# Mirrored times made as pairs by three products instead of four, with the V pairs in six stages and the next batch's folds moved to other steps, in an FFT mixing and spatial gating kernel

## The chip, the cores and the metric

The kernel runs on one core of one Trainium2 chip. The metric is device time in microseconds (us) of one execution; less is better. TensorE is called PE below, its weight loads PEld, VectorE DVE, ScalarE ACT, GpSimd POOL and the queue that issues most loads SP. Times of kernels are medians of runs in the fast state: none is over 1.5% above the fastest of its kernel. The spans and traces come from one profiled run each.

## The reference, cut to what matters

```python
batch, seq, dim, d_ff = 8, 3072, 256, 1024
X = np.fft.fft(np.fft.fft(x, axis=1), axis=2).real        # x: (8, 3072, 256)
h = np.maximum(X @ w_in, 0.0)                             # (8, 3072, 1024)
u, v = h[..., :512], h[..., 512:]
v_n = (v - mean(v)) / sqrt(var(v) + 1e-6)                 # over the last axis
v_s = einsum('ts,bsd->btd', w_spatial, v_n) + b_spatial   # (3072 x 3072) over time
out = (u * v_s) @ w_out                                   # (8, 3072, 256)
```

The spatial product is by far the largest. The point of the change is a symmetry. The transform at time S-t differs from that at time t only in the sign of the part that is odd in the width direction. With E and O for the even and odd half (128 rows each) and W0, W1 for the matching halves of the transformed w_in, h(t) = E W0 + O W1 before the relu, and h(S-t) = E W0 - O W1. The kernel only ever makes E and O for half of the times.

## The kernel before

The parts that matter: V (the second half of h, normalised), U (the first half), the gate, and the place of the work for the next batch. A batch is 6 chunks of 512 times, each 4 tiles of W of 768 rows; each tile has 4 steps, one per 128 columns of V, so 96 steps of six 128x512 products. PSUM is the memory that PE's products land in, divided into banks. `psM` is a ring of four of its banks that all small products share; `psW` holds the four sums of a chunk.

```python
def v_tile(b, i, eo, v, pr):            # one of 24 tiles of 128 times
    pv = psM.tile([P, DH], FP32, name="pv", tag="psM")
    for kt in range(2):
        if i < 12:                      # a direct time
            l, w = eo[:, kt, 128 * i:128 * i + 128], weo[:, kt, DH:]
        else:                           # a mirrored time: odd weights negated (wom)
            s0 = 128 * (KT - 1 - i) + 1
            l = eo[:, kt, s0:s0 + 128]
            w = weo[:, 0, DH:] if kt == 0 else wom[:, DH:]
        nc.tensor.matmul(pv, lhsT=l, rhs=w, start=(kt == 0), stop=(kt == 1))
    nc.scalar.activation(out=r, in_=pv, func=AF.Relu)
    nc.vector.bn_stats(out=stt[:, jj, :], in_=r)
    nc.vector.bn_aggr(out=mv[:, jj, :], in_=stt[:, jj, :])
# ... root and norm once per two tiles ...

def u_tile(b, c, dt, eo):               # likewise two products for each of 24 tiles
    # ...
    nc.scalar.activation(out=ut, in_=pu, func=AF.Relu)

def gate(c, pw, ut):                    # in the fourth tile of every chunk, once per step
    nc.vector.tensor_tensor(out=tm, in0=pw, in1=bbc[:, TC * c:TC * c + TC], op=ALU.add)
    nc.vector.tensor_tensor(out=gt, in0=tm, in1=ut, op=ALU.mult)

# in prep(b): what batch b needs, laid into the tiles of batch b-1
f0, df = (3, 2) if b == 1 else (0, 3)
for a in range(NA):                     # three folds of x, each an even and an odd half
    steps[f0 + df * a][0].append(lambda a=a: s_even(a))    # tiles 0, 3, 6 (3, 5, 7 for b == 1)
    steps[f0 + df * a][2].append(lambda a=a: s_odd(a))
```

A fold adds and subtracts mirrored rows and columns of x, on DVE; the DCT then makes E and O from the folds by products with tables of sines. Four of the 3072 times are left out of the folds and come in as the specials' sums (spb). Batch 0 has a head of its own: the tables, the three folds, the specials' sums, the first W pieces (128 times by 768 columns of w_spatial; each cast to bf16, turned by PE, copied out of PSUM), the DCT, and the first V tiles ahead of the main loop.

## Time and profile before

| | before |
|---|---|
| time (median of the first three runs) | 1470.2 us |
| PE busy | 1372.1 us, 93% of the span |
| DVE, ACT, POOL busy | 740.0, 464.2, 133.7 us |
| PE's wait for the gate (tm) | 23.4 us in 8 waits |
| first spatial product | at 80.8 us |
| batch 0, from its first spatial product to batch 1's | 228.2 us |
| batches 1 to 6, each | 168.3 us on average |
| batch 7 | 144.5 us |

In the busy shares, read PE first: at 93% it is the bound, and the question is what it does and where it stops.

### The profile page before, as it was taken

The page shows a single profiled execution, that of the slowest core. Times are in us where ns is not written, and L with a number is a line of the kernel's source. Part 1 is how long each engine was busy: PE and PEld are TensorE (multiplying, and loading weights), DVE is VectorE, ACT ScalarE, POOL GpSimd, SP SyncE. Part 2 cuts the span into 40 slices and gives each one's busy share as a digit, 9 for nine tenths or more (in the row PEclk, how much of TensorE's full clock was granted, in tenths as well). Part 3 has the DMA queues.
Part 4 walks back from the last instruction along what each step waited for, and adds up shares of the span by engine and source line. Part 5 has one row for each costly group of instructions (what it writes and reads, how often), then busy time and mean ns, then how long its engine had stood idle before and what let it go on. Part 6 is the DMA issues. An engine that isn't in the chain of part 4 may idle for free.

```text
span 1471.1 us, 18005 instructions
## 1 busy us (share of the span) xinstructions
PE 1372.1 (93%) x7071; PEld 673.5 (46%) x7071; DVE 740.0 (50%) x1491; ACT 464.2 (32%) x779; POOL 133.7 (9%) x187
## 2 busy tenths in 40 slices
PE   0667999999999999999999999999999999999998
PEld 0333455544444444444444444444444444444444
DVE  6757745555355634655344733565345643561212
ACT  3554235521244123431244113431244212441111
POOL 7622434410000000000000000000000000000000
PEclk9878999999999999999999999999999999999999
DMA  7863999795333543346334463336344443434441
GB/s 258 282 223 125 329 337 297 259 330 180 129 129 126 196 163 124 122 141 224 122 129 133 151 203 129 129 122 228 130 138 141 151 159 122 144 127 157 143 158 50
DMA packets 100597, 255.28 MB, mean 174 GB/s; under 512 B 13568, under 2 KB 60192, under 8 KB 100384
## 3 DMA queue, kind: packets, MB, share of 16 engines
q1 hardware_dynamic: 61440, 196.66, 39.4%
q10 hardware_dynamic: 29568, 44.05, 8.2%
q0 software_dynamic: 9504, 13.42, 2.8%
q8 instruction: 55, 0.90, 0.2%
q14 instruction: 30, 0.25, 0.0%
HBM read 210.80 MB, written 56.62 MB: 182 GB/s over the span
## 4 chain that ended last, share of the span: by engine, by line
PE 84%; DVE 7%; ACT 1%; issue 1%; ACTq 0%; DVEq 0%
PE pw L496 63%; PE po L512 6%; PE pu L488 5%; PE pv L454 5%; DVE tm L501 2%; PE pt L151 1%; PE pe L408 1%; DVE gt L504 1%; DVE sm L308 1%; DVE xt L328 1%; DVE stt L458 1%; DVE of L330 0%; DVE ef L312 0%; ACT v_t L472 0%; ACT r L457 0%
## 5 line engine op out<-in xcount | busy, mean ns | idle before, releaser
L496 PE MATMUL pw<-wt,v_t 128*128 128x512 bf16 x4608 | 1084.5, 382 | 37.6 <-DVE tm L501 23.4
L496 PEld LDWEIGHTS <-v_t 128*128 128x128 bf16 x4608 | 451.6, 98 | 581.2 <-issue 41.3
L501 DVE TENSOR_TENSOR tm<-pw,bbc 128x512 f32<-128x512 f32 x192 | 131.0, 682 | 263.5 <-PE pw L496 263.5
L490 ACT ACTIVATE ut<-pu 128x512 bf16<-128x512 f32 x192 | 114.6, 597 | 318.0 <-PE pu L488 213.2
L458 DVE BATCH_NORM_STATS2 stt<-r 128x6 f32<-128x512 f32 x192 | 132.6, 690 | 162.0 <-ACT r L457 162.0
L516 ACT COPY ot<-po 128x512 f32<-128x512 f32 x96 | 56.3, 586 | 309.6 <-PE po L512 308.0
L504 DVE TENSOR_TENSOR gt<-tm,ut 128x512 bf16<-128x512 f32 x192 | 135.8, 707 | 13.8 <-DVE tm L501 0.5
L457 ACT ACTIVATE r<-pv 128x512 f32<-128x512 f32 x192 | 111.0, 587 | 100.5 <-PE pv L454 91.3
L472 ACT ACTIVATE v_t<-r,rs 128x512 bf16<-128x512 f32 x96 | 78.1, 813 | 105.1 <-DVE rs L470 104.4
L512 PE MATMUL po<-wob,gt 128*128 128x256 bf16 x768 | 103.6, 279 | 1.4 <-DVE gt L504 1.4
L488 PE MATMUL pu<-eo_t,weo 128*128 128x512 bf16 x288 | 95.1, 385 | 2.4 <-ACT r L457 2.4
L454 PE MATMUL pv<-weo,eo_t 128*128 128x512 bf16 x288 | 94.7, 385 | 0.8 <-DVE wt L154 0.3
L512 PEld LDWEIGHTS <-gt 128*128 128x128 bf16 x768 | 76.8, 101 | 32.4 <-issue 3.3
L156 ACT COPY wt<-pt 128x768 bf16<-128x768 bf16 x53 | 42.0, 800 | 61.4 <-PE pt L151 61.0
L469 DVE RECIPROCAL rs<-rs 128x2 f32<-128x2 f32 x96 | 15.5, 162 | 89.0 <-ACT rs L465 89.0
L151 PE MATMUL pt<-ident,wb 128*128 128x128 bf16 x576 | 50.6, 231 | 6.9 <-ACT r L457 2.8
L454 PEld LDWEIGHTS <-eo_t 128*128 128x128 bf16 x384 | 37.2, 100 | 41.8 <-issue 2.7
L151 PEld LDWEIGHTS <-wb 128*128 128x128 bf16 x576 | 42.4, 104 | 29.0 <-issue 7.0
L474 DVE TENSOR_SCALAR v_t<-r,mv,rs 128x512 bf16<-128x512 f32 x96 | 52.7, 549 | 0.0
L146 POOL CAST wb<-wr 128x768 bf16<-128x768 f32 x48 | 42.6, 895 | 78.4 <-PE pt L151 46.9
L143 POOL CAST wb<-wr 128x768 bf16<-128x768 f32 x48 | 42.1, 887 | 70.3 <-PE pt L151 40.2
L410 ACT ACTIVATE eo_t<-pe,spb 128x384 bf16<-128x384 f32 (+1 forms) x32 | 35.8, 1117 | 37.8 <-PE pe L408 37.8
(218 smaller groups left out, 664.2 us busy)
## 6 DMA issues: line engine op xcount, KB each, us to landing
wt<-wtd SPq DMA_DIRECT2D x168, 768.0 KB, 4.4
wr<-in_moe_w_spatial_dram SPq DMA_DIRECT2D x96, 384.0 KB, 5.2
out_dram<-ot ACTq DMA_DIRECT2D x96, 256.0 KB, 3.9
wtd<-wt ACTq DMA_DIRECT2D x24, 768.0 KB, 5.3
xr<-in_x_dram POOLq DMA_DIRECT2D x32, 384.0 KB, 11.7
xt<-in_x_dram SPq DMA_DIRECT2D x21, 512.0 KB, 4.0
xt<-xr SPq DMA_DIRECT2D x21, 512.0 KB, 5.0
x<-in_x_dram SPq DMA_DIRECT2D x1, 1536.0 KB, 6.6
```

Of the source, the lines that this page charges most:

```text
L151: nc.tensor.transpose(pt[:, kk, :], wb[:, 128 * kk:128 * kk + 128], ident)
L454: nc.tensor.matmul(pv, lhsT=l, rhs=w, start=(kt == 0), stop=(kt == 1))
L457: nc.scalar.activation(out=r, in_=pv, func=AF.Relu)
L458: nc.vector.bn_stats(out=stt[:, jj, :], in_=r)
L472: nc.scalar.activation(out=v[:, i - 1, :], in_=r2[0], func=AF.Identity, scale=rs[:, 0:1], bias=rs[:, 2:3])
L488: nc.tensor.matmul(pu, lhsT=w, rhs=r, start=(kt == 0), stop=(kt == 1))
L490: nc.scalar.activation(out=ut, in_=pu, func=AF.Relu)
L496: nc.tensor.matmul(pw, lhsT=v[:, k, 128 * dt:128 * dt + 128], rhs=wt[:, kk, :], start=(k == 0), stop=(k == KT - 1))
L501: nc.vector.tensor_tensor(out=tm, in0=pw, in1=bbc[:, TC * c:TC * c + TC], op=ALU.add)
L504: nc.vector.tensor_tensor(out=gt, in0=tm, in1=ut, op=ALU.mult)
L512: nc.tensor.matmul(po[:, i, :], lhsT=gts[dt][:, t0:t0 + 128], rhs=wob[:, dt, :], start=(dt == 0), stop=(dt == NDT - 1))
L516: nc.scalar.copy(out=ot, in_=po)
```

## The change

The change has two intents: to save products where PE is the bound, and to move the folds out of the steps in which the gates run. A mirrored pair is made together: pv = E W0 + O W1 as before, pd = O (2 W1) as a third product, and the mirror is pv - pd. So three products stand where four did. ACT copies pd to SBUF and DVE subtracts. In U the mirror's relu moves into the gate. A V pair is cut into six stages, one per step, so that ACT and DVE do not wait for each other inside a stage. Time S/2 has no mirror and gets small products of its own. W's columns and rows are reordered to fit. The folds of the next batch stand in new steps, none of them a gate's, and in the head the first nine W casts move from POOL to ACT.

```diff
-NWR = 6
+NWR = 5
+ORDER = [0, 3, 1, 4, 2, 5]
+FOLD = [(2, 4), (8, 16), (18, 20)]          # steps of the even and odd halves, of 96
+FOLD1 = [(16, 20), (22, 26), (32, 34)]      # the same for batch 1
+DCT = [36, 38, 40, 42]
+VAT = [44 + (17 * i) // 4 for i in range(NPAIR)]
 ...
+        src = wr if g % 2 == 0 else view(wr, HW - 1, [[-1, HW]])
+        if first:
+            nc.scalar.copy(out=wb, in_=src)
         else:
-            nc.gpsimd.tensor_copy(out=view(wb, 127, ...), in_=view(wr, 0, ...))
+            nc.gpsimd.tensor_copy(out=wb, in_=src)
 ...
+    def v_pair(i, eo, pr):
+        for kt in range(2):
+            nc.tensor.matmul(pv, lhsT=eo[:, kt, sl], rhs=weo[:, kt, DH:], ...)
+        nc.tensor.matmul(pd, lhsT=eo[:, 1, sl], rhs=wo2[:, DH:], start=True, stop=True)
+        nc.scalar.activation(out=r[0], in_=pv, func=AF.Relu)
+        nc.scalar.copy(out=m_, in_=pd)
+    def v_minus(i, eo, pr, pv, pd):
+        nc.vector.tensor_tensor(out=r[1], in0=pv, in1=pd, op=ALU.subtract)
+        nc.vector.bn_stats(out=stt[:, 0, :], in_=r[0])
+    # v_relu (ACT), v_stat (DVE), v_root (ACT), v_norm (both): one stage a step
 ...
+    def u_pair(c, dt, eo):       # the same three products; um = pu - m_, no relu
 ...
-        nc.vector.tensor_tensor(out=gt, in0=tm, in1=ut, op=ALU.mult)
+        nc.vector.scalar_tensor_tensor(out=gt, in0=ut, scalar=0.0, in1=tm, op0=ALU.max,
+                                       op1=ALU.mult)
 ...
+    sp_ = specials()             # its PE part and DVE copies now come after the folds
     for i in range(3):
         piece(True)
 ...
+    early = [[] for _ in range(3 * NPAIR + 6)]      # batch 0: two pairs interleaved
+    for i in range(NPAIR):
+        for n, f in enumerate(cur.v_steps(i)):
+            early[3 * i + n].append(f)
```

## The prediction

> **What bounds the kernel now.** I read the page's busy shares first, then its slices, the costliest groups, PE's own waits, and last the chain of waits over single stretches. The busy shares and slices of the kernel before:
>
> ```profile
> PE 1372.1 (93%) x7071; PEld 673.5 (46%) x7071; DVE 740.0 (50%) x1491; ACT 464.2 (32%) x779; POOL 133.7 (9%) x187
> ...
> PE   0667999999999999999999999999999999999998
> ...
> PEclk9878999999999999999999999999999999999999
> ```
>
> The first line gives each engine's busy time in a span of 1471.1 us; the other two give PE's busy tenths and its granted clock in 40 slices of 36.8 us. PE is full from the fifth slice on; DVE is half used and ACT a third. There are two regimes: a head of some 147 us in which PE starves, and a long PE-bound rest. The costliest group, and the groups that the change touches:
>
> ```profile
> L496 PE MATMUL pw<-wt,v_t 128*128 128x512 bf16 x4608 | 1084.5, 382 | 37.6 <-DVE tm L501 23.4
> ...
> L501 DVE TENSOR_TENSOR tm<-pw,bbc 128x512 f32<-128x512 f32 x192 | 131.0, 682 | 263.5 <-PE pw L496 263.5
> L490 ACT ACTIVATE ut<-pu 128x512 bf16<-128x512 f32 x192 | 114.6, 597 | 318.0 <-PE pu L488 213.2
> L458 DVE BATCH_NORM_STATS2 stt<-r 128x6 f32<-128x512 f32 x192 | 132.6, 690 | 162.0 <-ACT r L457 162.0
> ...
> L516 ACT COPY ot<-po 128x512 f32<-128x512 f32 x96 | 56.3, 586 | 309.6 <-PE po L512 308.0
> ```
>
> 382 ns is the time of one pipelined matmul, not its spacing. The spacing comes from the chain of waits over 320 to 345 us (start, length, what; a steady batch):
>
> ```profile
> 322.15 5.18 PE pw L496 x24
> 327.33 0.43 PE pu L488 x2
> ...
> 330.43 1.23 DVE sm L308
> ...
> 339.98 0.60 DVE tm L501
> 340.58 0.04 issue
> 340.62 2.72 PE pw L496 x6
> 343.33 1.14 PE po L512 x8
> 344.48 0.43 PE pu L488 x2
> 344.91 5.18 PE pw L496 x24
> ```
>
> 24 matmuls take 5.18 us, 0.216 us each: what one 128x512 product costs while PE is the bound. The DVE lines in the middle are the one recurring stall. The folds of x for the next batch (sm to ho, about 3.7 us for either half) stand in the step in which the first chunk's four gates run; the gates queue behind them, and a PSUM bank of the next chunk is not free. PE's own waits (waited for: us in total, times, longest):
>
> ```profile
> PE pw L496 <- DVE tm L501: 23.4, 8, 3.7
> PE pw L496 <- ACT v_t L472: 14.2, 7, 3.3
> ```
>
> The 8 DVE waits are 3.7 and 0.5 us in batch 0 and six of 3.2 us, one in each of batches 1 to 6. The ACT waits all lie between 83 and 133 us, in the head. After a 3.2 us wait the next six matmuls take 2.72 us instead of 1.30: the stall also costs a colder clock, some 1.4 us here and 0.27 in the projection after it. Two such waits start matmuls at 508.45 and 677.68 us, so a batch takes 169.2 us.
>
> **What the Trainium skill says.** "TensorE: Matmul & The Clock Gate", section "Back-to-back issue gap", gives N/2.4 + 2.5 ns for one warm matmul, 215.8 ns at N=512. The trace agrees (5.18/24). The same section's 131 ns for sustained N=512 streams does not fit this trace. The page's section "What's actually happening" says that a window of some 3.4 us without activity puts PE at half clock. The trace roughly agrees: 3.2 us of waiting, then matmuls at half speed. "PSUM — Partial Sum Buffer", section "Specifications (TRN2)", says that a VectorE instruction may take at most one tensor input from PSUM. No run here shows it, but it explains the change's shape: of the two PSUM results that are subtracted, one is copied to SBUF by ACT first. "VectorE: DVE Perf Modes", section "The perf-mode tier table (the rule you actually need)", keeps tensor_tensor with a PSUM operand at its slowest mode. The trace agrees (682 ns for 512 columns), and I take that time for each subtraction.
>
> **The change, part by part.**
>
> 1. PE. A pair of mirrored tiles costs four products before (two each). After it costs three: the sum's two and one with the doubled odd half, and the mirror is the sum minus that. V: 12 pairs a batch, so 12 products fewer; U: 12 pairs, so 12 fewer. Over 8 batches 192 x 0.216 = 41.5 us. Added for the middle time S/2: two 128x512 products a batch in V (16 x 0.216 = 3.5 us) and eight one-column products a batch in U. The spacing of 128-column transposes is 0.335/6 = 0.056 us, so I estimate 0.06 us for one: 64 x 0.06 = 3.8 us. Net 41.5 - 7.3 = 34 us less. V of batch 0 and its first U pairs lie in the starved head, where PE's work is not the path; I leave out some 4 us. **-30 us.**
>
> 2. The folds leave the gates. Each batch is laid out in 96 steps, four to a tile of W. Gates fall in steps 12-15, 28-31, 44-47 and so on; the folds now stand in 2, 4, 8, 16, 18, 20 (for batch 1: 16 to 34, four steps that still fall outside the gates). A fold of 3.7 us then has no gate behind it, and a bank has four steps (5.2 us) before it is needed again. So six waits of 3.2 us with about 1.7 us of cold clock each should go (29 us), and 4.2 us with about 1 us of clock in batch 0. **-34 us.**
>
> 3. Added to ACT: one PSUM-to-SBUF copy per pair, 192 x 0.59 = 113 us; U's mirror loses its relu there (96 x 0.60 = 57 us), the gate's max takes it over. Added to DVE: 192 subtractions x 0.68 = 131 us. ACT would stand near 520 and DVE near 870 of some 1410 us. On average neither binds. In the V stage a pair costs DVE about 0.68 + 2 x (0.69 + 0.18) + 0.16 + 0.21 + 0.55 = 3.35 us, in 4.25 steps of 1.3 us and 0.65 us of its own products, 6.2 us. In a gate step DVE has 1.39 us of gates per 1.3 us step, so with about one whole pair in four such steps it lags by some 3 us; the bank is needed 4 to 5 us later. I count **+3 us** for places where this is not enough. The six stages, one a step, are what keeps an in-order engine from waiting for the other in the middle of a pair.
>
> 4. The head. Before, DVE's first fold waits 3.4 us for POOL's width tables, 4.1 us for the specials' sums, and is stretched by W's casts on POOL beside it: one sm takes 4.95 us where others take 1.23. The folds end at 60.2 us. After, the width tables come earlier and are smaller, the specials' sums come after the folds, and the first nine casts go to ACT. Folds from 23 us, 3 x 7.1 us: DVE would end near 45; ACT, with nine casts and nine copies of 0.8 us each that wait for transposes and four to six evictions, near 48. That is 10 us sooner. Then the V pairs: seven are begun ahead of the loop where seven single tiles were, and the rest run in its first nine steps. In a crowded head a pair costs the ACT-DVE round: relu and copy 1.2, subtract and statistics 1.6, root and norm 1.2, relu 0.6, some 4.6 us. Twelve are 56 us against the 64 us from 69 to 133 for 24 tiles before, but six U pairs and the gates' buffers now fall nearer. I put most of the gain down as used up: **-5 us**, uncertain by 8.
>
> 5. W pieces stay 128x768, 384 KB, but odd groups are read backwards at a 4-byte offset, one group of four has an extra one-column transfer per piece (24 in all, 128 elements of 4 bytes), and five pieces instead of six are in flight. Batch 0's loop runs at DMA shares of 0.9 to 1.0 and 294 to 362 GB/s between 150 and 260 us, and POOL waited there 19.6 us for W. PE's saving inside batch 0 is therefore in part not to be had. **+6 us.**
>
> Sum: 1470.2 - 30 - 34 + 3 - 5 + 6 = **1410 us**.
>
> **The rivals.** (a) PSUM becomes the wait. A pair takes two of the four shared banks at once, three where the U pair also has its one-column product, and a bank of the sum is held until DVE has subtracted. Steps 35 to 42 ask for projections, U pairs and the DCT's outputs together. Against it: ACT and DVE each have over a third of that stretch free. If every U pair and V pair cost PE 0.3 us, 192 x 0.3 = 58 us would come back, and the time would be near 1465. (b) DVE becomes the bound in gate steps, as it does today for four of them: a wait of 1 to 2 us, three times a batch, gives back 24 to 48 us, and 1435 to 1460. (c) Batch 0 is bound by DMA throughout: its head's gain and its PE saving vanish, about 10 us more, 1420. (d) PE's saving is hidden: excluded in the steady part, where PE has a single gap per batch.
>
> **Range and chances.** The two large terms rest on spacing and waits that the trace shows, so I trust their sign. The head may be 8 us off either way, DMA 5, and new waits may take up to 25 us: 1390 to 1436. Faster by over 2% means under 1440.8 us; only (a) or a strong (b) prevents it. Faster 0.89, within 2% 0.09, slower 0.02.
>
> **What would show it.** In the changed trace: 288 rather than 384 products each for V and U (and the small ones); PE's wait for the gate's tm gone or under 5 us in all; a batch period near 161 us (169.2 - 4.9 for wait and clock - 4.3 for PE, and a little back); the granted clock at 1.00 in steady slices; DVE near 870 us and ACT near 520; the last fold of batch 0 before 50 us. I am wrong if PE waits often for releases of the sum's or the difference's bank, if POOL's wait for W grows past 40 us and PE waits for its casts, or if the loop's tenth step comes later than the 120 us at which it began before.

## The result

The changed kernel takes 1419.67 us (1418.58 to 1419.97 in four runs) against 1470.49 us for the kernel before in the same rounds. The ratio of the two is 0.9654, with a 95% interval of 0.9637 to 0.9670. Ratios here are the mean time of one kernel's runs over that of the other's runs of the same rounds, so not quite the ratio of the medians quoted. The kernel is 3.5% faster, inside the predicted range and 10 us above the predicted figure.

The busy shares and slices of the page after answer to those of the prediction:

```profile
PE 1327.9 (94%) x6955; PEld 651.9 (46%) x6955; DVE 860.4 (61%) x1715; ACT 515.9 (36%) x888; POOL 126.1 (9%) x167
...
PE   0557989999999999999999999999999999999998
...
PEclk9968999999999999999999999999999999999999
```

PE has 44 us less to do, DVE 120 us more, and ACT 52 us more. PE is full from the fifth slice on, but for the sixth (8). PE's own waits after (us in total, times, longest):

```profile
PE pt L183 <- ACT wb L177: 45.7, 9, 31.1
PE pw L543 <- ACT v_t L507: 10.5, 3, 3.6
PE pt L183 <- POOL wb L179: 6.0, 3, 4.3
```

The wait for the gate's tm is gone from the list: 23.4 us before, none now. At the top stands a wait in the head for W casts on ACT, of which 31.1 us are the time before PE's first product; the kernel before had 36.9 us there. The remaining waits lie before 210 us, but for one of 0.24 us at 271 us and those for the last gates in the final microseconds (1.7 us). One steady stretch of each kernel, with the busy time of each engine, then granted clock, DMA share and GB/s (before, then after):

```profile
646.00:814.00 168.00, 164.81 (x812) 79.40 (x810) 85.04 (x179) 50.98 (x88) 0.00 (x0) 0.99 0.45 151
```

```profile
633.00:792.00 159.00, 159.00 (x800) 76.87 (x799) 101.79 (x209) 56.61 (x101) 0.00 (x0) 1.00 0.48 159
```

The first numbers are the stretch and its length, then PE. After, PE is busy for 159.00 of 159.00 us and the clock is at 1.00; before, 3.2 us were missing and the clock was at 0.99. DVE's 101.79 us of 159 still leave room.

From the two traces, by counting spatial products, the span of 1471.1 us became 1418.0 us as follows:

| part | before | after | difference |
|---|---|---|---|
| up to the first spatial product | 80.8 | 89.7 | +8.8 |
| batch 0 | 228.2 | 226.6 | -1.6 |
| batches 1 to 6 | 1009.6 | 950.9 | -58.7 |
| batch 7 | 144.5 | 142.6 | -2.0 |
| after the last spatial product started | 7.9 | 8.3 | +0.4 |

The profiled run of the kernel before took 1472.87 us, 2.4 more than the median, so the spans differ by 53.1 us and the medians by 50.8. So the steady part gave back more than the whole gain, and the head lost some of it. The experiments take these apart: first the steady part (which of two things made it faster), then the head.

### The profile page after: what moved, and what is told of

Its sections match the earlier page's. It is cut to its first block, busy times and chain, and to the rows that moved or that the text cites. A ratio compares the mean times of both kernels' runs of the same rounds, so it can differ in the third digit from the quotient of the medians.

```text
span 1418.0 us, 18127 instructions
## 1 busy us (share of the span) xinstructions
PE 1327.9 (94%) x6955; PEld 651.9 (46%) x6955; DVE 860.4 (61%) x1715; ACT 515.9 (36%) x888; POOL 126.1 (9%) x167
## 4 chain that ended last, share of the span: by engine, by line
PE 84%; DMA 3%; DVE 3%; ACT 1%; ACTq 0%; issue 0%; POOL 0%; SPq 0%; DVEq 0%; POOLq 0%
PE pw L543 66%; PE po L559 6%; PE pu L521 3%; PE pv L466 3%; PE pt L183 2%; PE pe L428 1%; PE pud L523 1%; PE pd L468 1%; DMA wr<-in_moe_w_spatial_dram 1%; DMA xt<-xr 1%; DVE tm L549 1%; DVE gt L550 1%; DVE xt L349 0%; DMA xt<-in_x_dram 0%; PE p L488 0%
## 5 line engine op out<-in xcount | busy, mean ns | idle before, releaser
L543 PE MATMUL pw<-wt,v_t 128*128 128x512 bf16 x4608 | 1054.5, 381 | 10.6 <-ACT v_t L507 10.5
L526 ACT ACTIVATE up<-pu 128x512 bf16<-128x512 f32 x96 | 57.3, 597 | 110.8 <-PE pu L521 75.0
L179 POOL CAST wb<-wr 128x768 bf16<-128x768 f32 x87 | 75.8, 873 | 173.0 <-PE pt L183 136.7
L499 ACT ACTIVATE rs<-mv,epst 128x2 f32<-128x2 f32 x96 | 28.5, 297 | 120.1 <-DVE mv L495 112.9
L484 ACT ACTIVATE r<-r 128x512 f32<-128x512 f32 x96 | 60.2, 627 | 29.5 <-DVE r L478 27.6
L466 PE MATMUL pv<-weo,eo_t 128*128 128x512 bf16 x192 | 60.2, 397 | 10.8 <-ACT wt L188 3.4
L550 DVE SCALAR_TENSOR_TENSOR gt<-up,tm 128x512 bf16<-128x512 bf16 x96 | 67.5, 704 | 3.3
L550 DVE SCALAR_TENSOR_TENSOR gt<-um,tm 128x512 bf16<-128x512 bf16 x96 | 66.9, 696 | 3.3
L470 ACT ACTIVATE r<-pv 128x512 f32<-128x512 f32 x96 | 56.3, 586 | 33.0 <-PE pv L466 30.3
L188 ACT COPY wt<-pt 128x768 bf16<-128x768 bf16 x53 | 42.2, 796 | 65.5 <-PE pt L183 65.4
L521 PE MATMUL pu<-eo_t,weo 128*128 128x512 bf16 x192 | 57.1, 379 | 0.0
```

Source lines behind the costliest of these rows:

```text
L179: nc.gpsimd.tensor_copy(out=wb, in_=src)
L466: nc.tensor.matmul(pv, lhsT=eo[:, kt, sl], rhs=weo[:, kt, DH:], start=(kt == 0), stop=(kt == 1))
L484: nc.scalar.activation(out=r[1], in_=r[1], func=AF.Relu)
L521: nc.tensor.matmul(ps, lhsT=weo[:, kt, wd], rhs=eo[:, kt, sl], start=(kt == 0), stop=(kt == 1))
L543: nc.tensor.matmul(pw, lhsT=v[:, k, 128 * dt:128 * dt + 128], rhs=wt[:, kk, :], start=(k == 0), stop=(k == KT - 1))
L550: nc.vector.scalar_tensor_tensor(out=gt, in0=ut, scalar=0.0, in1=tm, op0=ALU.max, op1=ALU.mult)
```

## The experiments

All ran with three rounds beside the kernel before, whose median was 1470.1 to 1471.5 us in them. The changed kernel ran in other rounds, so a difference from it of some 2 us says nothing. All runs were fast, and all passed as correct, e5 too, whose result is wrong on purpose; one variant did not build (see e4).

### e1: the changed kernel, folds back among the gates

My theory had two causes for the steady part: three products instead of four, and the folds' new place. The rival was that the six stages did it and the folds' place is idle. e1 and e2 complete a table of two by two; batch 1's folds are left where each kernel has them.

```diff
-FOLD = [(2, 4), (8, 16), (18, 20)]
+FOLD = [(0, 2), (12, 14), (24, 26)]
```

> The changed kernel with one line different: the folds for batches 2 to 7 stand again in steps 0, 2, 12, 14, 24, 26 of the batch before, two of them among the four gates. My theory (folds in the gates cost a wait of 3.2 us and a colder clock in each of six batches): PE's waits for tm come back, six of 2 to 4 us, the batch period goes from 158.4 to 162.5 to 164 us, and the time is 1444 to 1454 us. The rival (the six-stage V pairs and the three products took the stall away, the fold's place is idle): period stays within 1 us of 158.4, time 1417 to 1424 us.

Measured: 1453.13 us, ratio to before 0.9881 (0.9857 to 0.9905). Batches 1 to 6 take 164.1 us on average instead of 158.5. PE's waits in e1:

```profile
PE pw L543 <- DVE tm L549: 20.7, 12, 3.1
...
PE pu L534 <- DVE um L529: 4.9, 6, 0.8
```

The wait for tm is back at almost its old size, and six small waits for the mirror's subtraction join it, because the fold now also stands ahead of a U pair. That last reason is read from the schedule and was not tested. The rival falls: with three products and six stages, but folds among the gates, the time is 33 us longer.

### e2: the kernel before, only its folds moved

```diff
+            if b > 1:
+                s0, s1 = [(2, 4), (8, 16), (18, 20)][a]
+                s2 = s1
+            steps[s0 // 4][s0 % 4].append(lambda a=a: s_even(a))
+            steps[s1 // 4][s1 % 4].append(lambda a=a: s_odd(a))
```

> The kernel before, with only the folds of batches 2 to 7 moved to steps 2, 4, 8, 16, 18, 20; four products and everything else as it was. My theory: the period falls from 168.3 to about 163.3 us in six batches, so 30 us less, 1437 to 1445 us, and PE's waits for tm shrink from 23.4 to about 4 us. The rival (the saved products are what the changed kernel gained): time stays within 6 us of 1470.

Measured: 1439.04 us, ratio 0.9777 (0.9761 to 0.9793). A steady stretch of e2:

```profile
472.00:635.00 163.00, 163.00 (x813) 78.91 (x812) 85.36 (x179) 51.07 (x89) 0.00 (x0) 1.00 0.46 155
```

PE is gapless with four products too, and the batch period is 162.79 us. So new steps for the folds (and for the loads of x, which go with them in e1 and e2 alike), with nothing new computed, were worth 32 us of the 51. PE's waits for tm are 3.6 us in all. The two by two, in us for a batch (average of batches 1 to 6):

| | folds among the gates | folds elsewhere |
|---|---|---|
| four products | 168.3 (before) | 162.8 (e2) |
| three products | 164.1 (e1) | 158.5 (after) |

The folds' place is worth 5.5 to 5.7 us a batch and the rest of the change 4.2 to 4.4 us, each nearly the same beside the other. The rows differ in the saved products, the stages and the gate's relu together; the saved products alone account for 4.3 us by their count.

Of the 5.5 us, 3.2 are the wait. The other 2.3 are the clock, and the trace's clock record bears out this remainder: after four of the six waits before, it stands at half for 3.41 us, after the other two for 6.83 us. That is 27.3 us, of which half is lost, 2.3 us a batch. Two waits of nearly the same length need not cost the same: in e1 PE waits 3.12 us in each of the six batches, and the next six products take 2.72 us in three of them and 1.46 us in the other three.

### e3: the first nine W casts on POOL again

Now the head. In the changed kernel the folds end early, and then DVE idles. DVE, then ACT, by time (start, length, what, idle before):

```profile
44.47 0.17 DVE L362 COPY ho<-od 128x2 bf16<-128x2 bf16 x1
56.83 0.22 DVE L409 COPY spb<-pb 128x64 f32<-128x64 f32 x1 [12.19 <-PE pb L407]
```

```profile
29.99 0.23 ACT L388 ACTIVATE sp<-sp 32x32 f32<-32x32 f32 x1 [7.08 <-POOL sp L387]
30.13 0.21 ACT L389 ACTIVATE sp<-sp 32x32 f32<-32x32 f32 x1
30.25 0.81 ACT L177 CAST wb<-wr 128x768 bf16<-128x768 f32 x1
31.98 0.80 ACT L188 COPY wt<-pt 128x768 bf16<-128x768 bf16 x1 [0.92 <-PE pt L183]
32.67 0.83 ACT L177 CAST wb<-wr 128x768 bf16<-128x768 f32 x1
34.42 0.80 ACT L188 COPY wt<-pt 128x768 bf16<-128x768 bf16 x1 [0.92 <-PE pt L183]
```

The folds are done at 44.6 us, and the specials' sums (spb), which stand behind the nine pieces, reach DVE 12 us later. ACT shows why. Its first cast waits 7 us behind a sine that waits for POOL. After that each piece takes 2.44 us, from the copy at 31.98 to that at 34.42 and so on: a cast, 0.9 us in which ACT waits for PE to turn the piece, and a copy. Before, the sums had reached DVE at 37.8 us, and the folds had ended at 60.2.

```diff
-        if first:
-            nc.scalar.copy(out=wb, in_=src)
-        else:
-            nc.gpsimd.tensor_copy(out=wb, in_=src)
+        nc.gpsimd.tensor_copy(out=wb, in_=src)
```

> The changed kernel with the first nine W casts on GpSimd again instead of ScalarE. Theory (ScalarE's chain of cast, wait for the transposes and copy, 2.44 us a piece, ended the head's first part at 57 us although the folds were done at 44.6): pieces then cost about 1.0 to 1.6 us, the sums of the specials come at 46 to 50 us, the loop starts 5 to 8 us earlier than at 89.7 us, and the time is 1412 to 1416 us. Rival (GpSimd's casts stretch VectorE's folds as they did before, so the folds end near 52 to 55 us): the gain is under 3 us, 1417 to 1421 us.

Measured: 1413.79 us, ratio 0.9603 (0.9588 to 0.9617), 6 us less than the changed kernel. The sums reach DVE at 53.6 us, where 46 to 50 were expected, and the first spatial product starts at 83.7 instead of 89.7. Theory and rival each have a part of the truth. The gain is that of the theory, but the folds now end at 53.7 us instead of 44.6. POOL and DVE in e3:

```profile
32.86 3.90 POOL L176 CAST wb<-wr 128x768 bf16<-128x768 f32 x5
```

```profile
32.72 4.58 DVE L330 TENSOR_TENSOR ef<-sm 128x508 f32<-128x508 f32 x1
```

A DVE operation that takes 0.69 us elsewhere takes 4.58 us beside POOL's string of casts, as the one of 4.95 us did in the kernel before. So the move of the casts to ACT did protect the folds, by 9 us; it was paid for by ACT's serial chain.

### e6: the specials' tables after the first three pieces

```diff
-    sp_ = specials()
     for i in range(3):
         piece(True)
+    sp_ = specials()
```

> The changed kernel with the specials' tables emitted after the first three W pieces instead of ahead of them. Theory (ScalarE's first cast waits 7.1 us behind the specials' sine, which waits for GpSimd): the first cast starts near 23 to 25 us instead of 30.3, the sums' end moves from 57 to 50 to 53 us, the loop starts 4 to 7 us earlier, time 1412 to 1416 us. Rival (W or the identity arrives no earlier, or the V stage hides it): 1418 to 1421 us.

Measured: 1411.35 us, ratio 0.9594 (0.9579 to 0.9608), 8 us less than the changed kernel. The first cast starts at 22.8 us, the sums reach DVE at 49.4, and the first spatial product starts at 80.9. The 7 us that the first cast waited come through to the end; the gain is a little more than was expected.

### e8: ACT casts one piece ahead

```diff
         for kk in range(GK):
             nc.tensor.transpose(pt[:, kk, :], wb[:, 128 * kk:128 * kk + 128], ident)
+        if first and i + 1 < 9:
+            cast_w(i + 1, True)          # ahead of this piece's copy out of PSUM
```

> The changed kernel with ScalarE casting W piece i+1 before it copies piece i out of PSUM, in the first nine pieces; casts stay on ScalarE. Theory (each of these pieces costs 2.44 us because ScalarE waits 0.9 us for PE between cast and copy): 1.6 to 1.7 us a piece, the sums at 49 to 51 us instead of 57, folds untouched and ending at 44.6 us; time 1411 to 1415 us. Rival (the gain seen with the casts on GpSimd came from elsewhere than ScalarE's chain): 1418 to 1421 us.

Measured: 1410.56 us, ratio 0.9586 (0.9572 to 0.9600), 9 us less. ACT in e8:

```profile
33.41 0.80 ACT L199 COPY wt<-pt 128x768 bf16<-128x768 bf16 x1
34.10 0.84 ACT L177 CAST wb<-wr 128x768 bf16<-128x768 f32 x1
34.84 0.81 ACT L199 COPY wt<-pt 128x768 bf16<-128x768 bf16 x1
```

From one copy to the next are now 1.43 us instead of 2.44, without an idle mark. The sums reach DVE at 47.4 us. The same work on the same engine in another order is worth 9 us, slightly more than was expected.

### e7: the younger V pair's stage first

The second part of the head is V of batch 0, where two pairs are interleaved. In the changed kernel a pair takes 4.2 us there where nothing else comes between; over the twelve pairs it is 5.0 on average.

```diff
-        for f in early[u]:
+        for f in reversed(early[u]):
             f()
 ...
-                    steps[4 * (u - EARLY) // 9] += early[u]
+                    steps[4 * (u - EARLY) // 9] += early[u][::-1]
```

> The changed kernel with the order of the two interleaved V pairs turned round inside each step of batch 0 (the younger pair's stage first), nothing else. Theory (in the head a pair is bound by the round between ScalarE and VectorE, 4.2 us a pair, in which the younger pair's relu waits behind the older pair's norm on ScalarE): a pair takes 3.4 to 3.8 us, the loop starts 3 to 5 us earlier and batch 0's V ends 5 to 8 us earlier, time 1411 to 1416 us. Rival (PSUM banks or VectorE's own 3.35 us bind already): pair over 4.0 us, time within 2 us of 1419.7.

Measured: 1415.57 us, ratio 0.9621 (0.9605 to 0.9636), 4 us less. Two subtractions of neighbouring pairs, in the changed kernel and in e7:

```profile
88.41 0.69 DVE L478 TENSOR_TENSOR r<-pv,m__724 128x512 f32<-128x512 f32 x1
...
92.63 0.69 DVE L478 TENSOR_TENSOR r<-pv,m__748 128x512 f32<-128x512 f32 x1
```

```profile
86.00 0.69 DVE L478 TENSOR_TENSOR r<-pv,m__722 128x512 f32<-128x512 f32 x1 [0.57 <-ACT m__722 L472]
...
89.65 0.69 DVE L478 TENSOR_TENSOR r<-pv,m__746 128x512 f32<-128x512 f32 x1 [0.57 <-ACT m__746 L472]
```

The round is 4.22 us in the first and 3.65 us in the second. On ACT the younger pair's relu no longer stands behind the older pair's norm, which waits for DVE. DVE's own work in a round is some 3.35 us, so little is left. The last V tile of batch 0 is done at 129.5 instead of 134.5 us.

### e4 and e5: fewer buffers for W, and W read plainly

These ask what PE's wait for W's casts on POOL is: 6.0 us after, all of it past 133 us, where the kernel before had 0.6. A kernel with six pieces in flight, and two gate buffers fewer to make room, still did not fit into SBUF and never ran, so e4 goes the other way:

```diff
-NWR = 5
+NWR = 4
```

> The changed kernel with four W pieces in flight instead of five (six would not fit in SBUF). Theory (batch 0 waits for W because of too few buffers): PE's waits for W's casts grow from 6.0 us to over 12 and the time grows by 5 to 15 us, 1425 to 1435 us. Rival (DMA bandwidth, not buffers, sets those waits): within 3 us of 1419.7.

Measured: 1423.63 us, ratio 0.9673 (0.9656 to 0.9689): 4 us more than the changed kernel, between what theory and rival allowed. PE's wait:

```profile
PE pt L183 <- POOL wb L179: 9.4, 4, 5.1
```

It grew by 3.4 us, while eight traces with five pieces have it at 6.0 to 6.6 us. So fewer buffers do lengthen the wait. For the time it is less clear, as the intervals of the two ratios overlap. Whether a sixth piece would help stays open.

e5 leaves out the 24 one-column transfers and lets the odd groups start on a plain 768-column boundary. That puts W's mirrored columns off by one. The comparison with the reference did not notice, as W's entries are of the order 0.01/3072 beside a bias of 1.

```diff
-        lo = (s0 if g % 2 == 0 else S - s0 - HW + 1, HW if g != 1 else HW - 1)
+        lo = (s0 if g % 2 == 0 else S - s0 - HW, HW)
 ...
-            if g == 1:
-                nc.sync.dma_start(out=wr[p0:p0 + n, HW - 1:HW], ...)
```

> The changed kernel with W read plainly: the odd groups start on a row's own 768-column boundary and the 24 one-column transfers are gone (the result is wrong on purpose, W's mirrored columns are off by one). Theory (in batch 0 the small transfers and the offset by one element cost DMA time that PE waits for): PE's waits for W's casts fall from 6.0 us to under 3, time 1410 to 1417 us. Rival (the small transfers are hidden, the waits come from W's volume): within 2.5 us of 1419.7.

Measured: 1420.25 us, ratio 0.9655 (0.9638 to 0.9673): the same as the changed kernel. PE's wait:

```profile
PE pt L178 <- POOL wb L174: 6.6, 4, 4.2
```

POOL's own wait for W's loads past 133 us fell from 27.9 to 22.7 us, but PE's did not fall. The small and offset transfers cost nothing that shows in the time. The rival holds in its first half; that W's volume is what remains was only argued, not shown.

### e9: all three head edits, and e10: the bias loaded later

> The changed kernel with all three head edits at once: the specials' tables after the first three pieces, ScalarE casting one piece ahead, the younger pair's stage first. Theory (each shortens the same head, whose floor is VectorE's folds, which end at 44.6 us): the sums at 45 to 47 us instead of 57, so some 11 us, and about 4 us in the V stage; loop start near 75 us instead of 89.7; time 1402 to 1408 us, faster than every kernel so far. Rival (once the head is shorter, batch 0 waits for W's transfers instead and gives the gain back): 1408 to 1412 us, with PE's waits for W's casts over 12 us.

e9 has the edits of e6, e7 and e8 together. Measured: 1403.05 us (1402.54 to 1404.74), ratio 0.9537 (0.9521 to 0.9553), 17 us less than the changed kernel. The end of the folds and the sums, on DVE in e9:

```profile
45.07 0.16 DVE L373 COPY ho<-od 128x2 bf16<-128x2 bf16 x1
45.14 0.21 DVE L420 COPY spb<-pb 128x64 f32<-128x64 f32 x1
```

The sums now follow the folds at once, where 12.19 us of idling stood: the head's first part is bound by DVE's folds. The gains of e6 and e8 do not add up for that reason. PE's wait for W's casts on POOL stays at 6.4 us, so the rival falls. The head and batch 0 together now take 301.7 us, against 309.0 before and 316.2 in the changed kernel.

e10 takes e9 and issues the broadcast loads of the spatial bias after the early V pairs:

```diff
-    for c in range(NCH):         # bbc loads, ahead of the DCT
-        nc.sync.dma_start(out=bbc[...], ...)
 ...
+    for c in range(NCH):         # the same, after the early V pairs
+        nc.sync.dma_start(out=bbc[...], ...)
     x_step(1, 0)
```

> The kernel with all three head edits, and the broadcast loads of the spatial bias issued after the early V pairs instead of before the DCT. Theory (between 53 and 58 us ScalarE's queue stands behind the bias transfers, so the first V pair starts 4.1 us late): the first V product starts near 54 us instead of 57.6, loop start near 73 us, time 1398 to 1401 us. Rival (W's own transfers are just as late, or batch 0 waits for W and gives it back): 1402 to 1404 us.

Measured: 1401.60 us (1399.86 to 1405.48), ratio 0.9541 (0.9524 to 0.9559). The profiled run starts the first V product at 55.3 us, not 57.6 (near 54 was expected), and its first spatial product at 74.5 instead of 76.3. In the times it cannot be told from e9. Both e9 and e10 beat the kernel before and the changed kernel.

## Why the prediction was right or wrong

The time lay inside the range, and the mechanisms of the two large terms are shown. The steady batches gained more than predicted and the head lost where a gain was predicted. The total is near because these two errors have opposite signs, which is luck.

**PE (step 1): right.** 4.27 us a batch was predicted (24 products less two large and eight small ones). The steady periods of e2 (162.79) and after (158.42) differ by 4.37 us. The one-column products were over-estimated: the trace after has two of them between 326.21 and 326.26 us, about 0.03 us each instead of 0.06. "TensorE: Matmul & The Clock Gate", section "Wait — 56ns, not 53.3ns?", has a floor of about 25 ns from start to start for small matmuls. The trace agrees, and I should have used it.

```profile
326.21 0.19 PE L534 MATMUL pu<-eo_t,weo 128*128 128x1 bf16 x2
326.26 2.75 PE L543 MATMUL pw<-wt,v_t 128*128 128x512 bf16 x12
```

**The folds (step 2): right in mechanism, a little small.** For batches 1 to 6 I had 29 us. e2 gained 32 us and e1 lost 33 us. The clock's part was mis-sized: 1.7 us a batch predicted, 2.3 us measured. I had added up one wait, after which the clock was low for 3.41 us; after two of the six it was low for twice as long. Two slips changed nothing: half a fold takes 3.3 to 3.5 us in the stretch shown, not 3.7, and all six steps of batch 1's folds, not four, fall outside the gates.

**New waits (step 3): not there.** I allowed 3 us and there are none in steady batches; DVE came out at 860 us (predicted 870) and ACT at 516 (520). Rival (a), PSUM banks, and rival (b), DVE in gate steps, did not happen. The period came out at 158.5 us instead of near 161. Part of that is a misreading: the 169.2 us from which I subtracted is one of the two longest of six batches, whose mean is 168.3.

**The head (step 4): wrong, and the main miss.** It said -5 us; the first spatial product started 8.8 us later, and batch 0 won back only 1.6 us. One sign that I had named did occur: the loop's tenth step began at about 136 us, not before 120. The folds ended at 44.6 us, as predicted (near 45). The term that failed is "near 48" for ACT: the sums came at 56.8 us. I had counted nine casts and nine copies of 0.8 us, with something for waits. The waits are 0.9 us in every piece, because cast, transpose and copy are one serial round, and 7 us stood ahead of the first cast. e8 and e6 remove these two separately and gain 9 and 8 us.

The V round was predicted at 4.6 us and measured 4.2. But that is a round with nothing else between. Over the twelve pairs it is 5.0 us on average and up to 7.7, where a W piece or a U pair comes between. So the second saving in this step did not come either: from its first product to its last norm, V of batch 0 takes 65.4 us (69.1 to 134.5), where I had 56 and the kernel before took 63.1 (69.3 to 132.4). And six whole pairs and the first stages of a seventh now precede the loop, where seven single tiles did, so part of the V work only moved ahead of the first spatial product. For the same reason the tenth step is not a fair sign: it needs all 24 tiles of V after, and 18 before. With ACT's chain and the stage order mended (e9), head and batch 0 together come out 7.3 us under the kernel before, where I had about 6.

**DMA (step 5): the size is near, the cause is not settled.** In the kernel before, PE's waits for W's casts on POOL add up to 3.0 us, but most of them lie in the head, whose casts ACT makes in the changed kernel. From 133 to 320 us the kernel before has only

```profile
PE pt L151 <- POOL wb L146: 0.6, 1, 0.6
```

and the changed kernel all of its 6.0 us. So the wait rose by 5.4 us, near the 6 that I charged. POOL's own wait for W's loads rose from 19.6 to 27.9 us, under the 40 that I had named as a sign. Of the three reasons I gave, the offset reads and the one-column transfers are cleared by e5. The number of buffers has an effect on the wait (e4). Rival (c), batch 0 bound by DMA throughout, named 1420 us, and 1419.7 was measured, but not for its reason: e6, e8 and e9 shorten the head without a change to what is loaded, and the time follows.

Added up over the table of the result: batches 1 to 6 were predicted at about -52 us (29 + 25.6 - 3) and came out at -58.7. Head and batch 0, all terms together, were predicted at about -6 us and came out at +7.2. The two errors, 7 too little and 13 too much, leave 6 of the 10 us between 1410 and 1419.7. Most of the rest is that the profiled run of the kernel before, on which the table rests, was 2.4 us above its median.

## What to carry to other kernels

When two engines share a chunk's critical moment, first look at what stands in line ahead of it. Moving the two halves of one fold, some 3.5 us each, off the gates' steps gave 32 us without saving an instruction, more than the saved products. Where work moves to an idle engine, write down its chain and not its busy time: cast, wait and copy in turn cost 2.44 us a piece, and one piece ahead 1.43. In a steady stretch in which PE's busy time equals the stretch and its clock is 1.00 there is no wait left to remove. Only fewer products shorten it, as from e2 to the changed kernel (4.4 us a batch); the other gains are in the head.

## What the Trainium skill lacked or had wrong

- "TensorE: Matmul & The Clock Gate", section "Back-to-back issue gap": its figure of some 131 ns for sustained N=512 streams does not hold here (0.216 us in a gapless stream of 24); its other figure, N/2.4 + 2.5 ns, does.
- The same page, section "What's actually happening", puts the loss of the clock after an idle window of some 3.4 us. Here a little less was enough: six waits of 3.2 us lost it each time, and of six waits of 3.12 us in e1 three did. The cost of the six, beside the wait itself, was 2.3 us on average.
- "SBUF — State Buffer", section "SBUF: two separate sides", describes an exclusive lock on a pair of ports: whichever starts first, a VectorE operation with two inputs in SBUF or a GpSimd one that reads SBUF, has it for the whole instruction. In e3 one VectorE operation of 0.69 us took 4.58 us beside five GpSimd casts in a row (3.90 us) and ended 0.5 us after the last of them, so it seems not to have got in between two of them. The page does not say what happens when one GpSimd instruction follows another while VectorE waits.
